# An attention and MLP-mixer kernel: the second batch's loads issued ahead of Pool's casts, its copy of v on VectorE, and the first lists rearranged

## The chip, the cores and the metric

The kernel runs on one core of a Trainium2 chip. The metric is the device time of one execution in microseconds (us). The kernel before took 351.95 us, the median of three runs (349.81 to 352.16). Engines are named as in the profile: PE is TensorE (PEld its weight loads), DVE is VectorE, ACT is ScalarE, POOL is GpSimd, SP is the engine that in this kernel only issues DMAs. In the traces of this case each engine works through its own list of instructions in order, and an instruction that waits holds up all that stand behind it in that list: below, a copy on Pool whose input was ready at 21.9 us starts at 52.65 us, behind the list ahead of it, and holds PE's list for 21.4 us.

## The reference, cut to what matters

```python
def _attn_ref(q, k, v, global_idx):            # q, k, v: (8, 8, 576, 64) float32
    scores = scale * np.matmul(q, k.transpose(0, 1, 3, 2))
    mask = np.abs(pos[:, None] - pos[None, :]) <= 32
    mask = mask | is_global[:, None] | is_global[None, :]      # 8 global tokens
    scores = np.where(mask, scores, -1000000000.0)
    ...                                         # softmax over the row
    return np.matmul(attn, v)

def _moe_ref(x, w_tok1, w_tok2, w_ch1, w_ch2):  # x: (8, 576, 512)
    h = np.maximum(xt @ w_tok1, 0.0) @ w_tok2   # token mixer, xt = x transposed
    u = x + h.transpose(0, 2, 1)
    h2 = np.maximum(u @ w_ch1, 0.0) @ w_ch2     # channel MLP, 512 -> 1536 -> 512
    return u + h2
```

There are eight batches. Each goes through attention, the token mixer and the channel MLP.

## The kernel before

The kernel is a hand-made schedule. The order of the calls in the text is the order of each engine's list. Batch 0 runs alone at first (the start-up). From then on the channel MLP of batch b, which is dense work for PE, is mixed with the attention and token mixer of batch b+1 and the first steps of batch b+2. The first such stretch is "period 0": the channel MLP of batch 0, the attention of batch 1, the transposes of batch 2.

v is kept twice, as `vsh` and, shifted by 64 rows, as `vod` (the "odd copy"), because every second tile of 64 rows needs the shifted one. The helpers:

```python
    def load_v16(b):
        for c in range(NT):
            r0, r1, j0 = vrows(c)
            nc.gpsimd.dma_start(
                out=vsh[b % 2][r0:r1, c, :, 0:D],
                in_=v[b, :, j0 : j0 + (r1 - r0), :].rearrange("h p d -> p h d"),
            )

    def v_odd(b, hs=slice(0, H), eng=nc.gpsimd):
        i = b % 2
        eng.tensor_copy(out=vod[i][HQ:P, :, hs], in_=vsh[i][HQ:P, 0 : NT - 1, hs])
        eng.tensor_copy(out=vod[i][0:HQ, :, hs], in_=vsh[i][0:HQ, 1:NT, hs])

    def castv(p):
        hs = slice(2 * p, 2 * p + 2)
        nc.gpsimd.tensor_copy(out=vsh[0][:, :, hs, 0:D], in_=lv[:, :, hs])

    def cast_qk(b, ti, p, eng):

        if p is None:
            eng(out=(qr, kr)[ti][b % 2], in_=(lqr, lkr)[ti])
        else:
            hs = slice(2 * p, 2 * p + 2)
            eng(out=(qn, kn)[ti][b % 2][:, :, hs].rearrange("p i h d -> p h i d"), in_=(lq, lk)[ti][:, hs])
```

For batch 0 the work goes by pairs of heads. `PV0(p)` multiplies the weights of pair p with v, and needs `castv(p)` and the odd copy of that pair:

```python
    def PV0(p):
        s = st[0]
        ps = (pss if p % 2 else psv)([P, 2, 512], name=f"pv0_{p}")
        st[0]["pv", p] = ps
        spots = [(t, 64 * (t % 2)) for t in range(2 * NT - 1)] + [(2 * NT - 2, 64)]
        for t, r0 in spots:
            tau = t // 2
            lo = QS * tau + (NG + HQ if t % 2 else NG)
            for par in range(2):
                nc.tensor.matmul(
                    ps[r0 : r0 + 64, par, VW * tau : VW * tau + VW], lhsT=e_all[:, 2 * p + par, lo : lo + HQ],
                    rhs=(vod if t % 2 else vsh)[0][:, tau, 2 * p + par, :], start=t < 2, stop=False,
                )
        # ... the global part, out of lf and rf
```

The end of the batch-0 lists as the kernel before has them, with the block of Pool work for batch 1 in the middle. The odd copy of pair 3 (heads 6 and 7) stands behind that block in the text, but it is on VectorE, whose list has nothing of the block:

```python
    castv(2)
    load_wc1(0)
    v_odd(0, slice(2, 4), nc.vector)
    OG0(0)
    SX(0, 3, 1)
    OG0(1)
    RF0(0)
    v_odd(0, slice(4, 6), nc.gpsimd)
    LM(0)
    SX(0, 3, 0)
    OG0(2)
    RF0(2)
    PV0(0)
    RF0(1)
    castv(3)
    nc.gpsimd.memset(w2[:, :, S:], 0.0)
    load_wc1(4)
    load_wc1(8)
    load_qk1()
    load_wc2(0)
    qk_pads(1)
    v_ones(1)
    v_rows(1)
    x_pads(1)
    for p in (None, 0, 1, 2, 3):
        cast_qk(1, 0, p, G)
        cast_qk(1, 1, p, G)
    load_wc2(4)
    load_wc2(8)
    load_v16(1)
    v_odd(1)
    gather(1)
    PV0(1)
    NO0(0)
    OG0(3)
    v_odd(0, slice(6, 8), nc.vector)
    PV0(2)
    RF0(3)
    NO0(1)
    PV0(3)
    M1_0(0)
    NO0(3)
    M1_0(1)
    RU0(0)
    NO0(2)
    M2_0(0)
    RU0(1)
    # ... the rest of batch 0's token mixer, UT0(3), UT0(2), M2(0, 2), masks_a()
```

In period 0, `D` stands for the next unit of batch 0's channel MLP (`M4` is four b1p matmuls, `M5` six op matmuls), n is batch 1, m is batch 2:

```python
    def period_0():
        n, m = 1, 2
        D = None
        c2 = casts(m)
        u = [D, D, D, D, D, lambda: TR(n), D, lambda: globals_(n), lambda: t(n, 0), D]
        u += [lambda: t(n, 1), D, s2(n, 0), D, lambda: t(n, 2), lambda: SM(n, 0), D, s2(n, 1), D, lambda: t(n, 3)]
        u += [lambda: SM(n, 1), s2(n, 2), D]
        u += [D, lambda: SM(n, 2), lambda: GK(n), s2(n, 3), D, lambda: (load_rest(m), load_qk(m, slice(0, H)))]
        u += [lambda: SM(n, 3), D, lambda: OG(n), D, lambda: PV(n, 0), D, lambda: PV(n, 1), D]
        u += [lambda: PV(n, 2), lambda: [M1(n, ch) for ch in range(2)], lambda: PV(n, 3), D]
        u += [lambda: PV(n, 4), lambda: M1(n, 2), D, lambda: [M1(n, ch) for ch in range(3, NT)], *c2]
        u += [lambda: (M2(n, 0), M3(n, 0)), lambda: (M2(n, 1), M3(n, 1)), lambda: (M2(n, 2), M3(n, 2))]
        u += [lambda: (load_v16(m), v_odd(m)), lambda: globals_(m), lambda: TR(m)]
        u += [lambda p=p: t(m, p) for p in range(NP)]
        return u
```

The softmax here doesn't subtract the row's maximum and nothing guards it: scores larger than these inputs give would overflow.

## Time and profile before

| what | us | view |
|---|---|---|
| span of the profiled run | 351.7 | page |
| PE busy | 314.0 (89%) | busy time of each engine |
| first b1p matmul: batch 0's channel MLP starts, period 0 begins | 34.6 | timeline, PE |
| first b1p matmul of batch 1: period 0 ends | 89.2 | timeline, PE |

PE bounds the kernel: it is busy for 89% of the span and makes up 73% of the chain that ended last (page). Most of what can be saved lies in the first 90 us: in the table by stages PE is idle for about 24 us there, of 38 us in the whole span. These are lines of the page: busy share of 40 slices of 8.8 us in tenths, and under PEclk the clock granted to PE, in tenths of full speed.

```profile
PE 314.0 (89%) x3431; PEld 168.2 (48%) x3431; DVE 182.6 (52%) x380; ACT 154.4 (44%) x276; POOL 95.7 (27%) x125
...
PE   4799986773899999799998999899989999999993
...
POOL 8995564855204400530035000430000000000000
PEclk9589999997699999989999999999999999999999
```

PE's digits fall to 6, 7, 7 and 3 in the seventh to tenth slice (53 to 88 us), and the clock falls to 0.7 and 0.6 in the tenth and eleventh. The view of waits says for what. Its columns are: who waited, for whom, us in total, times, longest.

```profile
PE pT L398 <- DVE kT L436: 7.0, 5, 1.7
PE b1p L738 <- DMA uT<-u: 4.7, 1, 4.7
PE s L456 <- ACT kT L410: 2.6, 1, 2.6
PE warm L205 <- POOL ident masks.py:199: 2.0, 1, 2.0
PE pv L663 <- POOL vod L372: 1.9, 1, 1.9
```

Pool's timeline shows where batch 1 comes from. Columns: start, length, engine, line, instruction, and in brackets the idle time before it and what ended it.

```profile
26.39 0.94 POOL L367 DMA_DIRECT2D lk<-in_k_dram  x1
...
34.32 0.40 POOL L381 CAST qr<-lqr 128x256 f16<-128x256 f32 x1 [3.63 <-DMA lqr<-in_q_dram]
37.83 0.40 POOL L381 CAST kr<-lkr 128x256 f16<-128x256 f32 x1 [3.11 <-DMA lkr<-in_k_dram]
...
40.43 0.61 POOL L384 CAST kn<-lk 128x512 f16<-128x512 f32 x1 [1.64 <-DMA lk<-in_k_dram]
...
45.80 4.22 POOL L359 DMA_DIRECT2D vsh<-in_v_dram  x5
57.02 2.24 POOL L371 COPY vod<-vsh 64x2112 f16<-64x2112 f16 x1 [7.00 <-DMA vsh<-in_v_dram]
59.32 1.94 POOL L372 COPY vod<-vsh 64x2112 f16<-64x2112 f16 x1
```

Each cast runs as soon as its load has landed, from 34 us on. v of batch 1 is issued last and landed at 57 us, and Pool then copies it for 4 us while PE waits 1.9. At the end of period 0, PE waits 4.7 us for the DMA transposes of u. And the odd copy of batch 0's pair 3 is on VectorE, early:

```profile
26.36 0.48 DVE L371 COPY vod<-vsh 64x528 f16<-64x528 f16 x1
26.88 0.55 DVE L372 COPY vod<-vsh 64x528 f16<-64x528 f16 x1
```

### The profile page before, as it was taken

How to read it: one execution, taken by the hardware profiler on the slowest of the kernel's cores; microseconds unless marked ns; L12 is line 12 of the kernel's file. 1: busy time of each engine (PE TensorE's matmuls, PEld its weight loads, DVE VectorE, ACT ScalarE, POOL GpSimd, SP SyncE). 2: the span in 40 equal slices, each digit the busy share in tenths (PEclk: the TensorE clock that was granted, in tenths of full speed). 3: DMA queues.
4: the chain of work that ended last, by engine and by line, in shares of the span. 5: the costliest groups of instructions: out<-in, count | busy, mean ns of one | idle time of the engine just before them, and what ended most of it. 6: DMA issues, size and time to landing. Idle time of an engine off the chain costs nothing.

```text
span 351.7 us, 8081 instructions
## 1 busy us (share of the span) xinstructions
PE 314.0 (89%) x3431; PEld 168.2 (48%) x3431; DVE 182.6 (52%) x380; ACT 154.4 (44%) x276; POOL 95.7 (27%) x125
## 2 busy tenths in 40 slices
PE   4799986773899999799998999899989999999993
PEld 4468443432346554445454644444445645444641
DVE  5578464456244676556647474576656464241021
ACT  3654572051466335543365442563466433413600
POOL 8995564855204400530035000430000000000000
PEclk9589999997699999989999999999999999999999
DMA  7899699999909782929293922949100312042012
GB/s 212 190 178 264 162 130 158 289 91 137 260 10 89 199 203 63 88 43 302 77 108 38 278 91 63 99 147 227 62 2 15 76 63 61 0 104 91 0 67 85
DMA packets 82022, 42.37 MB, mean 120 GB/s; under 512 B 56578, under 2 KB 76674, under 8 KB 81986
## 3 DMA queue, kind: packets, MB, share of 16 engines
q1 hardware_dynamic: 43944, 31.20, 32.9%
q0 software_dynamic: 37904, 10.52, 28.2%
q8 instruction: 27, 0.44, 0.6%
q10 hardware_dynamic: 138, 0.13, 0.1%
q14 instruction: 9, 0.07, 0.1%
HBM read 36.11 MB, written 9.44 MB: 130 GB/s over the span
## 4 chain that ended last, share of the span: by engine, by line
PE 73%; DMA 9%; DVE 7%; POOL 7%; issue 2%; ACT 1%; SPq 0%; another core or an unknown queue 0%; POOLq 0%; ACTq 0%
PE op L764 25%; PE b1p L738 22%; PE a1p L690 4%; PE hp L710 4%; DMA lk<-in_k_dram 4%; PE s L456 4%; PE pv L654 3%; PE b1lp L751 3%; PE pT L398 3%; PE pv L663 2%; DMA vsh<-in_v_dram 2%; DMA uT<-u 2%; DVE x L677 2%; POOL kn L384 1%; PE og L537 1%
## 5 line engine op out<-in xcount | busy, mean ns | idle before, releaser
L738 PE MATMUL b1p<-uT,wc 128*128 128x512 f16 x384 | 97.6, 388 | 4.7 <-DMA uT<-u 4.7
L741 ACT ACTIVATE b<-b1p 128x512 f16<-128x512 f32 x96 | 56.9, 598 | 93.8 <-PE b1p L738 93.5
L764 PE MATMUL op<-wc,b 128*128 128x512 f16 x384 | 89.8, 380 | 0.0
L468 ACT ACTIVATE e_all<-s 128x544 f16<-128x544 f32 (+1 forms) x64 | 41.1, 685 | 40.7 <-issue 32.2
L359 POOL DMA_DIRECT2D vsh<-in_v_dram x35 | 29.5, 863 | 105.2 <-PE pv L663 98.2
L738 PEld LDWEIGHTS <-wc 128*128 128x128 f16 x384 | 34.8, 99 | 42.6 <-issue 8.3
L764 PEld LDWEIGHTS <-b 128*128 128x128 f16 x384 | 35.2, 98 | 38.9
L768 DVE TENSOR_TENSOR osb<-u,op 128x512 f32<-128x512 f16 x32 | 22.0, 687 | 55.1 <-PE op L764 52.5
L404 DVE COPY qT<-pT 128x512 f16<-128x512 f16 x31 | 21.3, 687 | 13.6 <-PE pT L398 12.7
L676 DVE RECIPROCAL rr<-pv 128x8 f32<-128x8 f32 (+1 forms) x35 | 7.3, 207 | 39.3 <-PE pv L663 36.6
L715 DVE TENSOR_TENSOR u<-x,hp 128x1024 f16<-128x1024 f16 x14 | 17.0, 1220 | 18.6 <-PE hp L710 18.6
L456 PE MATMUL s<-qT,kT 64*64 64x136 f16 (+2 forms) x704 | 19.0, 226 | 7.2 <-ACT kT L410 2.6
L479 DVE TENSOR_TENSOR e_all<-e_all,bandm 128x616 f16<-128x616 f16 x56 | 24.3, 476 | 1.0
L677 DVE TENSOR_TENSOR x<-pv,rr 128x512 f16<-128x512 f32 (+1 forms) x35 | 24.2, 691 | 1.2
L456 PEld LDWEIGHTS <-kT 64*64 64x64 f16 x704 | 12.2, 111 | 22.0 <-issue 16.1
L654 PE MATMUL pv<-rf,lf 128*64 128x264 f16 x126 | 19.1, 288 | 2.6 <-DVE x L677 1.8
L398 PE MATMUL pT<-ident,qn 128*128 128x128 f16 x128 | 13.3, 231 | 8.6 <-DVE kT L436 7.0
L710 PE MATMUL hp<-a,w 128*128 128x512 f16 x72 | 18.8, 379 | 1.6 <-ACT a L694 1.2
L663 PEld LDWEIGHTS <-e_all 128*64 128x64 f16 x504 | 18.5, 111 | 2.2 <-issue 2.1
L371 POOL COPY vod<-vsh 64x2112 f16<-64x2112 f16 (+1 forms) x8 | 14.5, 1816 | 17.6 <-DMA vsh<-in_v_dram 17.4
L410 DVE COPY kT<-pT 128x512 f16<-128x512 f16 x28 | 19.1, 681 | 0.0
L663 PE MATMUL pv<-vsh,e_all 128*64 128x66 f16 x280 | 18.8, 194 | 0.0
(170 smaller groups left out, 374.1 us busy)
## 6 DMA issues: line engine op xcount, KB each, us to landing
out_dram<-osb SPq DMA_DIRECT2D x32, 256.0 KB
lq<-in_q_dram SPq DMA_DIRECT2D x6, 1024.0 KB
lk<-in_k_dram SPq DMA_DIRECT2D x6, 1024.0 KB
wc<-in_moe_w_ch_dram POOLq DMA_DIRECT2D x6, 512.0 KB, 9.8
vsh<-in_v_dram POOLq DMA_DIRECT2D x21, 128.0 KB, 5.1
vsh<-in_v_dram POOLq DMA_DIRECT2D x14, 96.0 KB, 3.1
lq<-in_q_dram SPq DMA_DIRECT2D x4, 256.0 KB
lk<-in_k_dram SPq DMA_DIRECT2D x4, 256.0 KB
```

What stands on the lines that cost most here:

```text
L359: nc.gpsimd.dma_start(out=vsh[b % 2][r0:r1, c, :, 0:D], in_=v[b, :, j0 : j0 + (r1 - r0), :].rearrange("h p d -> p h d"),)
L398: nc.tensor.transpose(out=pT[:, ti, P * i : P * i + P], in_=n[b % 2][:, i, 2 * p : 2 * p + 2, :], identity=ident)
L456: nc.tensor.matmul(ps[o, par, i0 - a : i1 - a], lhsT=kT[r, HQ * j : HQ * j + HQ], rhs=qf[r, i0:i1], start=b > 0, stop=b > 0 or j in js[-2:],)
L468: nc.scalar.activation(out=e2[:, :, a:z], in_=ps[:, :, 0 : z - a], func=AF.Exp, scale=scale)
L479: nc.vector.tensor_mul(out=e2[:, par], in0=e2[:, par], in1=bm)
L654: nc.tensor.matmul(ps[r0 : r0 + 64, hf, 0 : NP * VW], lhsT=s["lf"][:, HQ * t : HQ * t + HQ], rhs=s["rf"][:, 2 * hf : 2 * hf + 2], start=Tr ...
L663: nc.tensor.matmul(ps[r0 : r0 + 64, hf, VW * hh : VW * hh + VW], lhsT=e_all[:, h, lo : lo + HQ], rhs=(vod if t % 2 else vsh)[b % 2][:, tau ...
L677: nc.vector.tensor_tensor(out=x16s[b % 2][r, tau, :].rearrange("p (f h x) -> p f h x", f=2, h=NP), in0=pq[r, :, :, 0:D], in1=rr[r].unsquee ...
L710: nc.tensor.matmul(ps[:, i, :], lhsT=w2[:, ch, P * tau - sh : P * tau - sh + P], rhs=s["a1"][:, ch, :], start=(ch == 0), stop=(ch == 1),)
L738: nc.tensor.matmul(ps, lhsT=wc1[:, cc, P * j : P * j + P], rhs=s["uT"][:, cc, :], start=(cc == 0), stop=(cc == 3))
L741: nc.scalar.activation(out=s["b1"][:, j, :], in_=ps, func=AF.Relu)
L764: nc.tensor.matmul(ps, lhsT=w, rhs=wc2[:, j, :], start=(j == 0), stop=(j == NJ - 1))
```

## The change

Its intent, as it was described: issue the second batch's loads early from Pool, ahead of its casts; do that batch's copy of v on VectorE; rearrange the first lists around data that arrives late. The core of the diff (cut; the start-up lists were reordered throughout, several memsets went from Pool to VectorE, some PSUM pools were swapped, and the odd copy of pair 2 went from Pool to VectorE, while that of pair 3 went the other way):

```diff
     load_qk1()
     load_wc2(0)
-    qk_pads(1)
+    load_wc2(4)
+    load_wc2(8)
     v_ones(1)
     v_rows(1)
+    load_v16(1)
     x_pads(1)
+    qk_pads(1)
     for p in (None, 0, 1, 2, 3):
         cast_qk(1, 0, p, G)
         cast_qk(1, 1, p, G)
-    load_wc2(4)
-    load_wc2(8)
-    load_v16(1)
-    v_odd(1)
     gather(1)
-    PV0(1)
-    NO0(0)
-    OG0(3)
-    v_odd(0, slice(6, 8), nc.vector)
-    PV0(2)
+    PV0(0)
+    NO0(1)
+    v_odd(0, slice(6, 8), nc.gpsimd)
+    OG0(3)
     # ... cut; PE: PV0(1), PV0(0), OG0(3), M1_0(1), PV0(3), M1_0(0), PV0(2), ...
```

And in period 0:

```diff
-        u += [D, lambda: SM(n, 2), lambda: GK(n), s2(n, 3), D, lambda: (load_rest(m), load_qk(m, slice(0, H)))]
-        u += [lambda: SM(n, 3), D, lambda: OG(n), D, lambda: PV(n, 0), D, lambda: PV(n, 1), D]
+        u += [D, lambda: SM(n, 2), lambda: GK(n), s2(n, 3), D, lambda: SM(n, 3), D, D, D]
+        u += [lambda: v_odd(n, eng=nc.vector), lambda: OG(n), D, lambda: (load_rest(m), load_qk(m, slice(0, H)))]
+        u += [lambda: PV(n, 0), lambda: PV(n, 1), D, lambda: PV(n, 2), lambda: PV(n, 3), D]
         # ... cut
+        u += [lambda: (M2(n, 0), M3(n, 0)), lambda: (M2(n, 1), M3(n, 1)), lambda: globals_(m), lambda: TR(m), lambda: t(m, 0)]
+        u += [lambda: (M2(n, 2), M3(n, 2)), lambda: (load_v16(m), v_odd(m)), lambda: t(m, 1), s2(m, 0), lambda: t(m, 2)]
+        u += [lambda: SM(m, 0), lambda: t(m, 3), s2(m, 1), lambda: SM(m, 1)]
```

More of the change, by code (lines that the diff above doesn't have):

```diff
@@ L119, in load_rest @@
         for ten, dst in ((q, lqr), (k, lkr)):
-            (nc.scalar if b == 0 and ten is q else nc.sync).dma_start(out=dst.rearrange("p i d -> p (i d)"), in_=rest_src(ten, b))
+            nc.sync.dma_start(out=dst.rearrange("p i d -> p (i d)"), in_=rest_src(ten, b))
     def load_v0(p):
@@ L134 @@
         load_qk(0, slice(2 * p, 2 * p + 2))
-        if p == 0:
+        if p == 1:
             load_rest(0)
@@ L158, in qk_pads @@
     def qk_pads(i):
-        nc.gpsimd.memset(kTs[i][:, :, 0:WIN], 0.0)
-        nc.gpsimd.memset(kTs[i][:, :, WIN + S :], 0.0)
+        nc.vector.memset(kTs[i][:, :, 0:WIN], 0.0)
+        nc.vector.memset(kTs[i][:, :, WIN + S :], 0.0)
     qk_pads(0)
-    nc.gpsimd.memset(qTs[0][:, :, :, 0:NG], 0.0)
+    nc.vector.memset(qTs[0][:, :, :, 0:NG], 0.0)
+    nc.vector.memset(lv[0:WIN, 0], 0.0)
+    nc.vector.memset(lv[P - WIN : P, NT - 1], 0.0)
     def int_op(name, s, op, s2=None, op2=ALU.bypass):
@@ L276 @@
     nc.gpsimd.iota(it_i, pattern=[[1, S]], base=0, channel_multiplier=0)
-    nc.gpsimd.memset(lv[0:WIN, 0], 0.0)
-    nc.gpsimd.memset(lv[P - WIN : P, NT - 1], 0.0)
     e_all = const.tile([P, H, ES], F16)
@@ L287, in v_ones, with v_rows @@
         nc.gpsimd.memset(vsh[i][:, :, :, D : D + 1], 1.0)
-    def v_rows(i):
-        nc.gpsimd.memset(vsh[i][0:WIN, 0], 0.0)
-        nc.gpsimd.memset(vsh[i][P - WIN : P, NT - 1], 0.0)
+    def v_rows(i, eng=nc.gpsimd):
+        xs = slice(D, D + 1) if i == 0 else slice(0, VW)
+        eng.memset(vsh[i][0:WIN, 0, :, xs], 0.0)
+        eng.memset(vsh[i][P - WIN : P, NT - 1, :, xs], 0.0)
     def x_pads(i):
@@ L394, in T @@
     def T(b, p):
-        pT = (psm if b == 0 else pss)([P, 2, 512], F16, name=f"pT_{b}_{p}")
+        pT = (psm if b in (0, 2) else pss)([P, 2, 512], F16, name=f"pT_{b}_{p}")
         for ti, n in enumerate((qn, kn)):
@@ L419, in TR @@
     def TR(b):
-        pr = (psm if b == 0 else pss)([P, 2, 4, NP * 16], name=f"pr_{b}")
+        pr = (psm if b in (0, 2) else pss)([P, 2, 4, NP * 16], name=f"pr_{b}")
         sel = ident.rearrange("p (n r x) -> p r n x", n=NP, r=2)
@@ L507, in GK @@
         s = st[b]
-        ps = (psv if b == 0 or b > 2 else pss)([P, 2, 512], name=f"gk_{b}")
+        ps = (psv if b != 2 else pss)([P, 2, 512], name=f"gk_{b}")
         for p in range(NP):
@@ L533, in OG @@
         s = st[b]
-        ps = (psv if b > 2 else pss)([P, 2, VW], name=f"og_{b}")
+        ps = (psv if b != 2 else pss)([P, 2, VW], name=f"og_{b}")
         for c in range(NT):
@@ L549, in OG0 @@
         s = st[0]
-        if p == 0:
+        if "rf" not in s:
             s["rf"] = mb.tile([P, NP, 2, VW], F16, tag="rf", name="rf_0")
@@ L600, in M1_0 @@
         s = st[0]
-        if p == 0:
+        if "a1" not in s:
             s["a1"] = mb.tile([P, 2, DM], F16, tag="a1", bufs=1, name="a1_0")
@@ L649, in PV @@
         tiles = ((2 * tau, 0), (2 * tau + 1, 64)) if tau < NT - 1 else ((2 * tau, sh),)
-        ps = (pss if b > 2 and tau % 2 else psv)([P, 2, 512], name=f"pv_{b}_{tau}")
+        ps = (pss if b != 2 and tau % 2 else psv)([P, 2, 512], name=f"pv_{b}_{tau}")
         def glob(hf):
@@ L786, in sparse2 @@
         u = [(0.0, lambda: (load_rest(n), load_qk(n, slice(0, H))))]
-        for p in range(NP):
+        for p in (2, 3):
             u += [(0.3, lambda p=p: S_(b, p, 0)), (1.8, lambda p=p: S_(b, p, 1)), (0.0, lambda p=p: SM(b, p))]
@@ L827, in period_0 @@
         u += [lambda: SM(n, 1), s2(n, 2), D]
-        u += [D, lambda: SM(n, 2), lambda: GK(n), s2(n, 3), D, lambda: (load_rest(m), load_qk(m, slice(0, H)))]
-        u += [lambda: SM(n, 3), D, lambda: OG(n), D, lambda: PV(n, 0), D, lambda: PV(n, 1), D]
-        u += [lambda: PV(n, 2), lambda: [M1(n, ch) for ch in range(2)], lambda: PV(n, 3), D]
-        u += [lambda: PV(n, 4), lambda: M1(n, 2), D, lambda: [M1(n, ch) for ch in range(3, NT)], *c2]
-        u += [lambda: (M2(n, 0), M3(n, 0)), lambda: (M2(n, 1), M3(n, 1)), lambda: (M2(n, 2), M3(n, 2))]
-        u += [lambda: (load_v16(m), v_odd(m)), lambda: globals_(m), lambda: TR(m)]
-        u += [lambda p=p: t(m, p) for p in range(NP)]
+        u += [D, lambda: SM(n, 2), lambda: GK(n), s2(n, 3), D, lambda: SM(n, 3), D, D, D]
+        u += [lambda: v_odd(n, eng=nc.vector), lambda: OG(n), D, lambda: (load_rest(m), load_qk(m, slice(0, H)))]
+        u += [lambda: PV(n, 0), lambda: PV(n, 1), D, lambda: PV(n, 2), lambda: PV(n, 3), D]
+        u += [lambda: PV(n, 4), lambda: [M1(n, ch) for ch in range(NT)], *c2]
+        u += [lambda: (M2(n, 0), M3(n, 0)), lambda: (M2(n, 1), M3(n, 1)), lambda: globals_(m), lambda: TR(m), lambda: t(m, 0)]
+        u += [lambda: (M2(n, 2), M3(n, 2)), lambda: (load_v16(m), v_odd(m)), lambda: t(m, 1), s2(m, 0), lambda: t(m, 2)]
+        u += [lambda: SM(m, 0), lambda: t(m, 3), s2(m, 1), lambda: SM(m, 1)]
         return u
@@ L880 @@
     A, V, G = nc.scalar.copy, nc.vector.tensor_copy, nc.gpsimd.tensor_copy
+    consts()
     W(10)
@@ L884 @@
     W(20)
-    consts()
-    cast_qk(0, 0, 0, A)
-    cast_qk(0, 1, 0, A)
-    cast_qk(0, 0, None, V)
+    cast_qk(0, 0, 0, V)
+    cast_qk(0, 0, 1, A)
+    cast_qk(0, 1, 0, V)
+    gather(0, (0,))
+    masks_b()
+    masks_c()
     T(0, 0)
+    TEq(0, 0, A)
+    cast_qk(0, 1, None, A)
+    TEk(0, 0, A)
+    cast_qk(0, 1, 1, V)
     gather(0, (1,))
-    masks_c()
-    TEq(0, 0, V)
-    TEk(0, 0, A)
-    cast_qk(0, 0, 1, A)
-    cast_qk(0, 1, 1, V)
+    v_ones(0)
+    nc.gpsimd.memset(w1l, 0.0)
+    v_rows(0, nc.vector)
+    cast_qk(0, 0, 2, V)
+    cast_qk(0, 0, None, A)
+    T(0, 1)
+    masks_d()
+    cast_qk(0, 1, 2, A)
+    TR(0)
+    TEq(0, 1, V)
+    TEk(0, 1, A)
     S_(0, 0, 0)
+    TRE(0, (0,), A)
+    TRE(0, (1,), V)
+    S_(0, 1, 0)
     SX(0, 0, 0)
-    gather(0, (0,))
-    v_ones(0)
-    v_rows(0)
-    nc.gpsimd.memset(w1l, 0.0)
-    T(0, 1)
-    cast_qk(0, 0, 2, V)
-    masks_b()
-    TEk(0, 1, A)
-    TEq(0, 1, A)
-    cast_qk(0, 1, None, A)
-    S_(0, 1, 0)
-    cast_qk(0, 1, 2, G)
-    TR(0)
-    masks_d()
-    SX(0, 1, 0)
-    G(out=g16[1][0], in_=g32[1][0])
-    T(0, 2)
-    TRE(0, (1,), V)
-    TRE(0, (0,), A)
-    castv(0)
+    G(out=g16[0][0], in_=g32[0][0])
+    T(0, 2)
+    load_w1()
+    load_w1l()
+    load_w2()
+    SX(0, 1, 0)
     S_(0, 1, 1)
-    TEq(0, 2, V)
-    TEk(0, 2, A)
+    TEk(0, 2, V)
     S_(0, 0, 1)
@@ L923 @@
     cast_qk(0, 0, 3, V)
-    G(out=g16[0][0], in_=g32[0][0])
-    load_w1()
-    load_w1l()
-    load_w2()
     cast_qk(0, 1, 3, V)
+    SX(0, 0, 1)
+    TEq(0, 2, V)
+    T(0, 3)
+    G(out=g16[1][0], in_=g32[1][0])
+    TEq(0, 3, A)
+    TEk(0, 3, V)
+    S_(0, 2, 0)
+    castv(0)
     gather_t(0)
-    SX(0, 0, 1)
-    S_(0, 2, 0)
+    S_(0, 2, 1)
+    SX(0, 2, 0)
     GTE(0)
+    castv(1)
     GKE(0)
-    T(0, 3)
-    SX(0, 2, 0)
-    v_odd(0, slice(0, 2), nc.vector)
-    S_(0, 2, 1)
-    TEk(0, 3, A)
-    TEq(0, 3, V)
     SX(0, 2, 1)
     GQ0()
-    castv(1)
+    v_odd(0, slice(0, 2), nc.vector)
+    v_odd(0, slice(2, 4), nc.vector)
     GK(0)
@@ L950 @@
     load_wc1(0)
-    v_odd(0, slice(2, 4), nc.vector)
-    OG0(0)
     SX(0, 3, 1)
     OG0(1)
-    RF0(0)
-    v_odd(0, slice(4, 6), nc.gpsimd)
-    LM(0)
-    SX(0, 3, 0)
-    OG0(2)
-    RF0(2)
-    PV0(0)
-    RF0(1)
+    LM(0)
+    OG0(0)
+    RF0(1)
+    SX(0, 3, 0)
+    v_odd(0, slice(4, 6), nc.vector)
+    OG0(2)
+    PV0(1)
+    RF0(2)
+    RF0(0)
     castv(3)
@@ L975 @@
         cast_qk(1, 1, p, G)
-    load_wc2(4)
-    load_wc2(8)
-    load_v16(1)
-    v_odd(1)
     gather(1)
-    PV0(1)
-    NO0(0)
-    OG0(3)
-    v_odd(0, slice(6, 8), nc.vector)
-    PV0(2)
-    RF0(3)
-    NO0(1)
+    PV0(0)
+    NO0(1)
+    v_odd(0, slice(6, 8), nc.gpsimd)
+    OG0(3)
+    RF0(3)
+    M1_0(1)
+    NO0(0)
     PV0(3)
+    RU0(1)
     M1_0(0)
     NO0(3)
-    M1_0(1)
+    PV0(2)
     RU0(0)
+    M2_0(0)
     NO0(2)
-    M2_0(0)
-    RU0(1)
     M1_0(3)
     M2_0(1)
+    RU0(3)
     AD0(0)
-    RU0(3)
     M1_0(2)
@@ L1005 @@
     AD0(3)
+    M2_0(2)
+    UT0(0)
     M3_0(1)
-    UT0(0)
-    M2_0(2)
+    AD0(2)
     UT0(1)
-    AD0(2)
     M3_0(3)
```

## The prediction

> **What bounds it now.** TensorE: busy 314.0 of 351.7 us (engine table); the chain of waits is 73% PE. From about 100 us on there is little idle. The slack lies in the start-up (batch 0 alone, up to the first channel-MLP matmul at 34.6 us in the timeline) and in period 0 (34.6 to 89.2 us, where the second batch's channel MLP starts). In period 0 the timeline shows 1.9 us waiting for Pool's copies of v (57.0 to 61.3 us, two of about 1.94 us), batch 2's transposes at VectorE's pace (78.7 to 84.5 us), 4.7 us waiting for the DMA transposes of u, then some 5 us at a granted clock of 0.72 to 0.77 (stage table).
>
> **What the change intends.** v of batch 1 (landed only at 57 us) is issued before Pool's casts; its odd copy goes to VectorE; batch 2's transposes and first scores fill the wait for the u transposes. This should recover roughly 2 us (Pool copy) plus 5 to 8 us (u wait, clock dip, transposes).
>
> **What I think it breaks.** The last odd copy of batch 0's v (pair 3) was on VectorE, at 26.4 us. Now it is on Pool, behind everything for batch 1: the wc2 and v loads, ten casts, four gathers. Pool runs in order, and PE's in-order list needs this copy for PV0(3), before the rest of batch 0's mixer. Waits ahead of it in Pool's list: [...] the copy for the gathers to land.
>
> Costs from the trace: k of batch 1 is issued at 26.4 us and lands at 40.4; Pool skips about 5 us of small work but VectorE's memsets delay the gather index, so perhaps 39 us now. Casts: 5.3 us, to about 45. Bytes: the wc2 loads and v (4.3 MB read) follow k; two wc2 loads plus v took 44.3 to 57 us, about 255 GB/s, so wc2 lands near 50 and v near 55. Gathers took about 4.5 us to land: 55 to 57. Copy 1.3 us: PV0(3) can finish near 57.5 us instead of 28.
>
> PE is then idle from roughly 26 to 57 us. In before, PV0(3) to first channel-MLP matmul took 7.1 us; I allow 8[...]. [...] So that matmul moves from 34.6 to about 65.5 us. Period 0 then finds its data: I estimate 45 to 47 us instead of 54.6, including 1.5 us of batch 2's scores moved in. The second batch's channel MLP starts near 111 instead of 89.2; minus the moved work and the vanished clock dip, net about +18 us. All after is PE-bound and unchanged, so this is nearly all critical.
>
> **Prediction:** 370 us, 8 in 10 between 359.5 and 381. Faster by over 2%: 0.04; within 2%: 0.07; slower by over 2%: 0.89.
>
> **What would show it.** Right: PE idle 20 to 30 us, released by Pool's 64x528 vod copy; that copy after the casts and gathers, at 50 us or later; first b1p matmul after 57 us; period 0 under 50 us; no 4.7 us wait for uT. Wrong: the vod copy or the first b1p matmul before 45 us.
>
> **What would make it wrong.** [...] period 0 compressing more once its data is there; or a longer stall, if gathers are served slowly after all v packets.

The copy's end near 57.5 us (gathers landed at 55 to 57, plus 1.3; that the gathers come only after the landings of wc2 and the first of v is the author's estimate, with its reason cut) plus 8 is 65.5 us for the first b1p. With 45 to 47 us of period 0 that gives about 111 instead of 89.2, or +22; less the moved work (1.5) and the clock dip (it has no figure of its own; about 2 is what is left for it), +18; and 352 + 18 is 370 us.

## The result, and the profile after

The changed kernel took 374.99 us (median of 4 runs, 372.39 to 376.37) against 350.88 us for the kernel before in the same rounds (349.57 to 352.16). The ratio is 1.068, with a 95% interval of 1.060 to 1.076. Ratios here are the mean time of one kernel's fast runs over the mean of the other's fast runs in the same rounds, so not quite the ratio of the quoted medians. The output is correct.

The same lines of the page, now for slices of 9.3 us:

```profile
PE 318.1 (86%) x3431; PEld 173.5 (47%) x3431; DVE 186.0 (50%) x393; ACT 153.4 (41%) x275; POOL 87.7 (24%) x113
...
PE   5695019989858998997999899989998999999994
...
POOL 6885755301240350035003500250000000000000
PEclk9999999999989999999999999999999999999999
```

PE has a hole (0 and 1) in the fifth and sixth slice that was not there before. The waits of PE name it:

```profile
PE pv L578 <- POOL vod L373: 21.4, 1, 21.4
PE pT L399 <- DVE kT L437: 6.3, 4, 1.7
PE pT L399 <- ACT kn L385: 3.9, 1, 3.9
```

The 4.7 us wait for uT and the 1.9 us wait for the full odd copy are gone, as intended. One wait of 21.4 us has come. Pool's timeline shows how it arises:

```profile
25.75 0.92 POOL L368 DMA_DIRECT2D lk<-in_k_dram  x1
...
35.88 1.77 POOL L360 DMA_DIRECT2D vsh<-in_v_dram  x2 [1.70 <-DMA lq<-in_q_dram]
39.48 0.78 POOL L360 DMA_DIRECT2D vsh<-in_v_dram  x1 [1.83 <-DMA lk<-in_k_dram]
...
40.77 0.40 POOL L382 CAST qr<-lqr 128x256 f16<-128x256 f32 x1
...
50.04 0.94 POOL L236 DMA_INDIRECT g_k<-in_k_dram,idx_i  x1 [0.30 <-issue]
52.65 0.62 POOL L372 COPY vod<-vsh 64x528 f16<-64x528 f16 x1 [1.66 <-DMA g_k<-in_k_dram,idx_i]
53.33 0.62 POOL L373 COPY vod<-vsh 64x528 f16<-64x528 f16 x1
```

The copy of pair 3, 1.3 us of work whose input was cast by 21.9 us, starts at 52.65 us. Everything for batch 1 stands ahead of it. Two things in that list are worth a look. Pool stood idle for 1.83 us before the last issue of v, and the trace puts that down to the landing of k, which this issue does not read; the 1.70 us before the two issues ahead of it are put down to q in the same way. Why an issue of v waits for them is in no trace. The casts behind these issues, whose first input had landed at 34 us in the kernel before, therefore start only at 40.8 us. And the trace puts the last 1.66 us of idle time before the copy down to the gathers' data, although the copy reads none of it.

PE's timeline on both sides of the hole:

```profile
32.31 0.32 PE L578 MATMUL pv<-vsh,e_all 128*64 128x66 f16 x2
54.00 0.21 PE L578 MATMUL pv<-vod,e_all 128*64 128x66 f16 x1 [21.37 <-POOL vod L373]
```

and the two b1p matmuls that mark the ends of period 0, with the wait before the second:

```profile
64.80 4.52 PE L739 MATMUL b1p<-uT,wc 128*128 128x512 f16 x20
...
106.21 0.50 PE L399 MATMUL pT<-ident,kn 128*128 128x128 f16 x4 [3.92 <-ACT kn L385]
112.10 1.04 PE L739 MATMUL b1p<-uT,wc 128*128 128x512 f16 x4
```

| stretch | before | after | difference |
|---|---|---|---|
| start to first b1p | 34.6 | 64.8 | +30.2 |
| period 0 | 89.2 - 34.6 = 54.6 | 112.1 - 64.8 = 47.3 | -7.3 |
| the rest of the span | 351.7 - 89.2 = 262.5 | 370.6 - 112.1 = 258.5 | -4.0 |
| span of the profiled run | 351.7 | 370.6 | +18.9 |

So the new period 0 does gain: 7.3 us in itself, and 4.0 us in the rest. (The rest probably gains because some of batch 2's scores are already done, and because no slow clock follows: the record of the kernel before is 0.77 between 90 and 100 us, right after its period 0, that of the changed kernel 1.00 between 110 and 140 us. Neither share was measured.) The start-up loses 30.2 us, of which the hole is 21.4. The other 8.8 us do not come from the hole: e1 below has no hole, and its first b1p still comes 9.0 us later than in the kernel before. The profiled run, at 372.39 us, was also the fastest of the four. By the medians the loss is 24.1 us; what the slower runs lose beyond the table's 18.9 us is in no trace.

### The profile page after: what moved, and what is told of

It reads as the page before. It is cut to its first block, busy times and chain, and to the rows that moved or that the text cites. A ratio compares the mean times of both kernels' runs of the same rounds, so it can differ in the third digit from the quotient of the medians.

```text
span 370.6 us, 8086 instructions
## 1 busy us (share of the span) xinstructions
PE 318.1 (86%) x3431; PEld 173.5 (47%) x3431; DVE 186.0 (50%) x393; ACT 153.4 (41%) x275; POOL 87.7 (24%) x113
## 4 chain that ended last, share of the span: by engine, by line
PE 71%; DVE 4%; issue 4%; DMA 3%; ACT 2%; SPq 1%; ACTq 0%
PE op L765 23%; PE b1p L739 22%; PE hp L711 4%; PE a1p L691 4%; DMA lk<-in_k_dram 3%; PE s L457 3%; PE pT L399 3%; PE b1lp L752 3%; PE pv L655 3%; PE pv L664 2%; DVE x L678 1%; PE a1p L612 1%; ACT e_all L469 1%; PE og L538 1%; PE hp L625 1%
## 5 line engine op out<-in xcount | busy, mean ns | idle before, releaser
L739 PE MATMUL b1p<-uT,wc 128*128 128x512 f16 x384 | 94.7, 380 | 0.5 <-ACT b L742 0.5
L411 DVE COPY kT<-pT 128x512 f16<-128x512 f16 x30 | 20.4, 680 | 1.5 <-PE pT L399 0.8
L578 PE MATMUL pv<-vod,e_all 128*64 128x66 f16 x32 | 2.6, 245 | 21.4 <-POOL vod L373 21.4
L655 PE MATMUL pv<-rf,lf 128*64 128x264 f16 x126 | 18.9, 287 | 0.9 <-DVE kgz L354 0.7
```

The costliest lines, as they stand in the source:

```text
L655: nc.tensor.matmul(ps[r0 : r0 + 64, hf, 0 : NP * VW], lhsT=s["lf"][:, HQ * t : HQ * t + HQ], rhs=s["rf"][:, 2 * hf : 2 * hf + 2], start=Tr ...
L739: nc.tensor.matmul(ps, lhsT=wc1[:, cc, P * j : P * j + P], rhs=s["uT"][:, cc, :], start=(cc == 0), stop=(cc == 3))
```

## The experiments

The theory: the time is lost because the odd copy of pair 3 stands on Pool behind the work for batch 1. The rivals: the early loads disturb the loads that matter; the new start-up lists or VectorE's memsets are slow in themselves; Pool is simply too slow an engine for the copy. All twelve kernels gave the right output. The kernel before was run beside each. "Median" is over all runs of the kernel; the ratio uses fast runs alone. One run of the kernel before, in the rounds of e5 to e8, took 1687.22 us; it counts as slow and is in no ratio. The profiled runs of e2, e8, e11 and e12 are slow.

| run | what it is | median us (before, same rounds) | ratio, 95% interval |
|---|---|---|---|
| e1 | changed kernel, pair-3 copy back on VectorE | 353.59 (352.33) | 0.996, 0.984 to 1.008 |
| e2 | changed kernel, copy on Pool but early in its list | 353.62 (352.33) | 1.003, 0.994 to 1.011 |
| e3 | changed kernel, copy just ahead of the gathers | 370.15 (352.33) | 1.048, 1.036 to 1.060 |
| e4 | kernel before, only the copy moved to Pool | 384.73 (352.33) | 1.088, 1.078 to 1.098 |
| e5 | e1, batch 2's load at its old place | 349.96 (351.08) | 0.998, 0.993 to 1.002 |
| e6 | e1, more warm-up matmuls | 351.81 (351.08) | 1.003, 1.000 to 1.007 |
| e7 | old start-up, early loads, new period 0, batch 2's load at its old place | 348.92 (351.08) | 0.997, 0.992 to 1.001 |
| e8 | kernel before, early loads and VectorE copy only | 350.80 (351.08) | 1.001, 0.996 to 1.006 |
| e9 | e7, v issued after the casts | 342.63 (352.05) | 0.973, 0.967 to 0.980 |
| e10 | e8, v issued after the casts | 345.08 (352.05) | 0.983, 0.977 to 0.989 |
| e11 | changed kernel, PE kept busy in the hole | 374.05 (352.05) | 1.061, 1.051 to 1.070 |
| e12 | e5, v issued after the casts | 347.69 (351.38) | 0.976, 0.969 to 0.984 |

### e1 to e4: is it the place of one copy?

e1, one word:

```diff
-    v_odd(0, slice(6, 8), nc.gpsimd)
+    v_odd(0, slice(6, 8), nc.vector)
```

> The changed kernel with one word undone: the odd copy of batch 0's v for heads 6 and 7 goes back to VectorE. Theory (the copy's place in Pool's queue is the cause): the 21.4 us wait of PE for Pool's vod copy vanishes, the first b1p matmul moves from 64.8 us to 40 to 44 us, and the time falls to about 350 us (345 to 355), level with the kernel before, because the rest of the change still loses a little in the start-up and in the 3.9 us wait for batch 2's k. Rival (the early loads of wc2 and v, or the memsets put on VectorE, slow the first 60 us by contention): the time stays above 360 us.

e2, the same copy on Pool, moved up:

```diff
     castv(3)
+    v_odd(0, slice(6, 8), nc.gpsimd)
     nc.gpsimd.memset(w2[:, :, S:], 0.0)
     # ...
     NO0(1)
-    v_odd(0, slice(6, 8), nc.gpsimd)
```

> The changed kernel; the copy for heads 6 and 7 stays on Pool but stands right behind the cast of its own v, ahead of the loads for batch 1. Theory (place in the queue, not the engine): same time as the run with the copy on VectorE, within 3 us, since it costs Pool only 1.3 us. Rival (Pool is the wrong engine for this copy): the time stays within 5 us of the changed kernel, 370 us or more.

e3, moved up past the gathers only:

```diff
         cast_qk(1, 1, p, G)
+    v_odd(0, slice(6, 8), nc.gpsimd)
     gather(1)
     PV0(0)
     NO0(1)
-    v_odd(0, slice(6, 8), nc.gpsimd)
```

> The changed kernel; the copy for heads 6 and 7 moves up past the four gathers only, still behind the loads and casts of batch 1. Theory: the copy starts when the casts end, near 46 us instead of 52.65, so the time falls by about 6.5 us, to 368 us; every microsecond of the copy is a microsecond of the kernel. Rival (the copy is held by the v loads and not by its place): no change, 374 us.

e4, the kernel before with the opposite one-word edit (`nc.vector` to `nc.gpsimd` in the same call):

> The kernel before with one word changed: the copy for heads 6 and 7 goes to Pool at the place where the text has it, behind the casts, the loads, the full odd copy of batch 1 and the gathers. Theory: PE waits for it until about 71 us instead of 28; period 0 then finds its data and shrinks from 54.6 to about 45 us; the time rises by 30 to 38 us, to about 385 us. Rival (the word is harmless and the new order of lists or the early loads did the damage): less than 358 us.

Measured: e1 and e2 are both level with the kernel before. Moving this one copy undoes the whole net loss of 6.8%, and the engine is not the reason: on Pool, early in the list, it costs the kernel no more than on VectorE (1.003 against 0.996, with intervals that overlap). In e1 the 21.4 us wait is gone and the first b1p matmul stands at 43.6 us. In e3 the copy starts at 45.30 us, 7.35 us earlier than in the changed kernel, and PE's wait is 7.4 us shorter:

```profile
45.30 0.62 POOL L372 COPY vod<-vsh 64x528 f16<-64x528 f16 x1
45.99 0.62 POOL L373 COPY vod<-vsh 64x528 f16<-64x528 f16 x1
```

```profile
PE pv L578 <- POOL vod L373: 14.0, 1, 14.0
```

How far the time fell is not sharp, because the two kernels ran in different rounds: the medians fell by 4.8 us (374.99 to 370.15), the ratios by 2.0 points (1.068 to 1.048), which is about 7 us. A fall of 6.5 was expected, and both agree with it within the intervals. In the profiled run the first b1p came only 5.1 us earlier (59.67 against 64.80), since PE then took 13.0 us instead of 10.8 from its restart to that matmul. So "every microsecond of the copy is a microsecond of the kernel" is not shown. e4 rose by 32.4 us (384.73 - 352.33), inside the 30 to 38 that were expected, with this wait of PE:

```profile
PE pv L577 <- POOL vod L372: 41.4, 1, 41.4
```

As causes of the net loss the rivals fall. The early loads, memsets and lists of e1 are those of the changed kernel, and it does not lose. That its start-up costs nothing is not shown: it ends 9.0 us later than in the kernel before, and the rest of the kernel makes up for that.

### e5 and e6: what still eats the gain once the copy is mended?

e1 has the shorter period 0 and is still only level. Two suspects stood in its profile: PE waits 4.2 us for ACT's cast of batch 2's k, and the start-up ends at 43.6 instead of 34.6 us.

e5, on top of e1:

```diff
-        u += [D, lambda: SM(n, 2), lambda: GK(n), s2(n, 3), D, lambda: SM(n, 3), D, D, D]
-        u += [lambda: v_odd(n, eng=nc.vector), lambda: OG(n), D, lambda: (load_rest(m), load_qk(m, slice(0, H)))]
+        u += [D, lambda: SM(n, 2), lambda: GK(n), s2(n, 3), D, lambda: (load_rest(m), load_qk(m, slice(0, H))), lambda: SM(n, 3), D, D, D]
+        u += [lambda: v_odd(n, eng=nc.vector), lambda: OG(n), D]
```

> The changed kernel with the pair-3 copy on VectorE, and with the load of batch 2's q and k put back to the place where the kernel before has it (ahead of the last mask of period 0, not behind the copy and the global output). Theory: the 4.2 us wait of PE for ACT's cast of batch 2's k is the load being issued late (k issued about 12 us before it lands); it vanishes and the time falls by 3 to 5 us against the run with the copy on VectorE, to about 349.5 us. Rival (that wait only hides another, VectorE's or the DMA transposes): less than 1.5 us gained.

e6, on top of e1:

```diff
-    W(10)
+    W(32)
     indices()
     # ...
     S_(0, 0, 0)
+    W(22)
     TRE(0, (0,), A)
```

> The changed kernel with the pair-3 copy on VectorE, and with 44 more warm-up matmuls in two waits of the start-up (22 before the index matmul, 22 while PE waits for the second k transpose). Theory [...]: the batch-0 matmuls take about 0.20 instead of 0.25 us from 15 us on, the first b1p matmul moves from 43.6 us to 37 to 39 us, the time falls by 4 to 6 us, to about 348.5 us. Rival (the slow clock costs nothing because VectorE and ACT set the pace there): b1p moves by less than 1.5 us.

Measured for e5: the wait is gone from the profile, and batch 1's channel MLP starts at 88.7 instead of 94.2 us. The time, 349.96 us, is what was expected, but the ratio of 0.998 overlaps that of e1, so a gain over e1 is not shown by the timed runs. In the changed kernel the load stands behind two more writes of the output in SP's list, and k is issued 12 us before the cast of it starts; in the kernel before, 17 us (58.99 to 76.18).

Measured for e6 (`W(n)` issues n matmuls whose result nobody reads): the matmuls were faster. These lines are the last `pv<-rf` group of batch 0 and the first b1p matmuls, from e1 and from e6:

```profile
35.59 0.87 PE L586 MATMUL pv<-rf,lf 32*128 32x66 f16 x12
43.57 2.80 PE L739 MATMUL b1p<-uT,wc 128*128 128x512 f16 x12
```

```profile
30.92 0.60 PE L586 MATMUL pv<-rf,lf 32*128 32x66 f16 x12
36.30 4.52 PE L739 MATMUL b1p<-uT,wc 128*128 128x512 f16 x20
```

The same twelve matmuls take 0.87 us in e1 and 0.60 in e6, and the first b1p comes 7.3 us earlier (36.3 against 43.6). So batch 0 had run at a slow clock in e1: in e3 such groups of 0.87 us stand beside a clock record of 0.50 (20 to 30 us), in the kernel before those of 0.60 us beside one of 1.00 (20 to 30 us). What made it slow is not shown; the expectation's statement on batch 0's clock and its cause is cut. That the added matmuls made the others faster is not shown either. e11 below has the changed kernel's PE list, without them, up to its filler. Its trace and the changed kernel's agree within 0.03 us for each matmul up to 18 us; then, by the length of its groups, one runs at the full clock and the other does not. These are the first such groups of the changed kernel and of e11:

```profile
28.18 0.87 PE L586 MATMUL pv<-rf,lf 32*128 32x66 f16 x12
```

```profile
25.31 0.60 PE L586 MATMUL pv<-rf,lf 32*128 32x66 f16 x12
```

So the same list can run at either clock, and e1 and e6 have one trace each. The time did not follow in e6: 351.81 us, ratio 1.003. PE now reached batch 1's data before Pool had cast it, and waited 1.5 us for the cast of q's rest and still 3.9 for batch 2's k; batch 1's channel MLP started 5.1 us earlier in the profiled run (89.1), and that run was the fastest of the six. Why the timed runs do not show those 5 us is open; that some of e1's other runs had the full clock too would explain it, but none of them has a trace.

### e7 to e10: the parts of the change on the old start-up

e7 keeps the start-up of the kernel before and takes the rest of the change, with the load of batch 2 where it was:

```diff
-    qk_pads(1)
+    load_wc2(4)
+    load_wc2(8)
     v_ones(1)
     v_rows(1)
+    load_v16(1)
+    qk_pads(1)
     x_pads(1)
     # ... the ten casts
-    load_wc2(4)
-    load_wc2(8)
-    load_v16(1)
-    v_odd(1)
     gather(1)
     # and period_0() as in e5, with the PSUM pools that it needs
```

> The kernel before, its start-up lists kept; only the early loads on Pool, the copy of batch 1's v on VectorE and the new period 0 are taken from the change, with the load of batch 2 at its old place. Theory (the new start-up order is what eats the gain of the new period): first b1p at 34.6 us as before, batch 1's channel MLP starts at 80 to 83 us instead of 89.2, and the time is 343 to 347 us, better than both kernels. Rival (the early loads or the new period 0 lose as much as they gain): 350 us or more.

e8 makes the same edit to Pool's list and puts `v_odd(n, eng=nc.vector)` ahead of `OG(n)`, with the lists of period 0 as they were:

> The kernel before with only the early loads of wc2 and v on Pool and the copy of batch 1's v on VectorE; both lists as before. Theory: PE's 1.9 us wait for Pool's copy of v vanishes, the 4.7 us wait for the DMA transposes of u stays; 349 to 351 us, 1 to 3 us below the kernel before. Rival (v issued before the casts delays the casts of batch 1, and period 0 with them): same or slower than before.

e7 missed its expectation (0.997). e8's 350.80 us lies in the expected 349 to 351, but the expected gain over the kernel before is absent (1.001), which is what its rival said. The profile of e7 says why. PE has a new wait of 4.0 us for Pool's cast of the rest of q, and Pool's timeline shows what holds that cast:

```profile
36.66 1.75 POOL L359 DMA_DIRECT2D vsh<-in_v_dram  x2 [2.39 <-DMA lq<-in_q_dram]
40.59 0.78 POOL L359 DMA_DIRECT2D vsh<-in_v_dram  x1 [2.18 <-DMA lk<-in_k_dram]
...
42.28 0.40 POOL L381 CAST qr<-lqr 128x256 f16<-128x256 f32 x1
```

The last issue of v came only when k had landed, after 2.18 us of idle time, and the casts stand behind it. v itself is issued earlier (at 32 to 41 instead of 46 to 50 us), but the casts come 8 us later (34.32 to 42.28). Hence e9, which is e7 with this:

```diff
     v_ones(1)
     v_rows(1)
-    load_v16(1)
     # ...
         cast_qk(1, 1, p, G)
+    load_v16(1)
     gather(1)
```

> As the run with the old start-up and the new period 0, but on Pool batch 1's v is issued after the ten casts (the wc2 loads still before them). Theory (the v issues block Pool until k has landed, one after the other, and so hold the casts of q that could have run earlier): PE's 4.0 us wait for Pool's cast of the rest of q falls below 1 us; v still lands before the copy on VectorE needs it; batch 1's channel MLP starts at 82 to 84 us instead of 86.6; 344 to 347 us, and clear of the kernel before by over 1%. Rival (the wait is for the landing of q itself, or v now lands too late): no gain over the run with v before the casts (0.997 of before).

and e10, which is e8 with the same edit:

> As the last, with the lists of period 0 left as the kernel before has them: only the two wc2 loads move ahead of the casts, v follows the casts directly, and the copy of batch 1's v is on VectorE. Theory: the 5.9 us wait for the cast of the rest of q falls below 1 us; the 1.9 us wait for Pool's copy is gone; the 4.7 us wait for the transposes of u stays; 348 to 350 us. If it equals the run with the new period, the new lists of period 0 are worth nothing.

e9 took 342.63 us against 352.05, a ratio of 0.973: the best version found, better than both kernels, though its interval reaches just over 0.980. Pool's timeline in e9 has the first cast back at its load's landing and v issued right behind the casts:

```profile
33.82 0.40 POOL L381 CAST qr<-lqr 128x256 f16<-128x256 f32 x1 [0.53 <-DMA lqr<-in_q_dram]
...
43.87 4.20 POOL L359 DMA_DIRECT2D vsh<-in_v_dram  x5
```

The copy of v on VectorE then takes 1.4 us, where Pool took 4, and PE no longer waits for it:

```profile
59.03 0.71 DVE L371 COPY vod<-vsh 64x2112 f16<-64x2112 f16 x1
59.77 0.70 DVE L372 COPY vod<-vsh 64x2112 f16<-64x2112 f16 x1
```

Batch 1's channel MLP starts at 79.83 us, 9.4 earlier than in the kernel before, and the time is 9.4 us lower (352.05 - 342.63). e10, at 0.983, did better than expected (345.08 instead of 348 to 350 us). So moving the two wc2 loads ahead of the casts, v right behind them and the copy to VectorE is worth 1.7%; the new lists of period 0 add about 1 point on top, a difference that the two intervals just leave open.

### e11: does the slow clock after the hole cost anything?

```diff
     NO0(0)
+    fill = psm([P, P], name="fill")
+    for _ in range(320):
+        nc.tensor.matmul(fill, lhsT=ident, rhs=ident, start=True, stop=True)
     PV0(3)
```

> The changed kernel as it is, with 320 warm-up matmuls put into PE's list right where it waits 21.4 us for the copy. Theory (part of the loss is that batch 0's rest runs at half clock after the idle time): the stretch from the copy to the first b1p matmul, 10.8 us, falls to 7 to 8 us, and the time to about 371.5 us. Rival (the rest of batch 0 is paced by VectorE and ACT): under 1 us gained.

Inconclusive for the time. The filler was over at 45.8 us in the profiled run, PE then idled 8.3 us, and the matmuls behind the hole were as slow as before, with a clock record of 0.50 between 50 and 60 us:

```profile
54.92 0.87 PE L586 MATMUL pv<-rf,lf 32*128 32x66 f16 x12
```

The same groups had taken 0.60 us ahead of the filler in this run, so here idle time of PE was followed by a slow clock. In the changed kernel it need not have been the hole: there the groups take 0.87 us at 28.18 us already, before it. The time, ratio 1.061 against 1.068, is not apart from the changed kernel's. What the slow clock costs there can be read from e1 and e6, which have the same PE list in this stretch: from the last `pv<-rf` group to the first b1p matmul, 43.57 - 35.59 = 8.0 us in e1 and 36.30 - 30.92 = 5.4 us in e6.

### e12: is the new start-up to blame?

e12 is e5 with the edit of e9, so that it differs from e9 in the start-up alone.

> The changed kernel with all three defects mended: the pair-3 copy on VectorE, the load of batch 2 at its old place, v of batch 1 after the ten casts on Pool. It differs from the best version so far (2.7% below the kernel before) in the start-up lists, memsets and first loads alone. Theory (the new start-up lists are the part of the change that loses once the copy is mended, because the first b1p matmul comes at 43 to 44 us instead of 35): no better than the run with two defects mended, 349 to 351 us, a ratio to before of 0.99 to 1.00; casts-first gains nothing here, since batch 1's transposes are not asked for before 48 us. Rival (the start-up lists cost little and v's place did it all): 344 us or less.

The expectation was missed. The ratio of the fast runs is 0.976, and that is not apart from e9. The seven runs fall into two groups: three at 341.57 to 342.25 us, and four at 347.69 to 349.84, which count as slow. In these three fast runs the new start-up is as good as the old one, so the theory that it must eat the gain fell. But a run is called slow here because it is over 1.5% above the fastest of its kernel; over all seven runs the mean is 345.8 us, against 350.8 for the kernel before. The profiled run was a slow one (first b1p at 42.8 us, matmuls of 0.87 us as in e1). That the fast runs are those in which PE gets its full clock early is a guess, since none of them has a trace. It fits that e11's trace shows the changed kernel's start-up list at the full clock, and that the means of the two groups lie 6.8 us apart, near the 7.3 us by which the first b1p of e6 precedes that of e1. The clocks do not settle it: 0.988 to 0.993 in the fast runs; 0.950, 0.951, 0.969 and 0.994 in the slow ones. If the guess holds, leaving the slow runs out flatters the new start-up. What stays open is also how much of e5's 350 us, in runs that are all called fast by their own kernel's best, was this same slow start.

## Why the prediction was right

- **The step that carried it held.** The prediction said that the copy of pair 3 on Pool stands "behind everything for batch 1" and that PE waits for it "20 to 30 us". PE waited 21.4 us; with the copy back (e1, e2), the loss was gone. Alone in the kernel before (e4), the same word cost 32.4 us.
- **The queue was longer in the sum than in fact.** Predicted: gathers landing at 55 to 57 us and PV0(3) able to finish near 57.5. Measured: the copy began at 52.65 and PE went on at 54.0. The landing of wc2 was put too late: "near 50". Its three loads took 14.9 to 16.8 us from issue, the last of them from 29.87 us, so all had landed by about 47. The gathers, which the prediction put after it, were issued from 46.1 us on, and of the 0.16 to 0.31 us of idle time before each of them the trace puts none down to a load.
- **The rest of batch 0 was underrated.** "I allow 8": from PE's restart to the first b1p it took 64.8 - 54.0 = 10.8 us. Part is the slow clock (8.0 against 5.4 us for a piece of it in e1 and e6). Another part may be the new order, in which PE waits before PV0(3) with the mixer steps of pairs 0 and 2 and PV0(2) still to do; this was not measured apart. The two errors nearly cancel, which is luck: 64.8 us against the predicted 65.5.
- **Period 0** was 47.3 us against "45 to 47". It held a 3.9 us wait for batch 2's k, which the prediction did not see: the load had moved behind two more output writes in SP's list. With the load moved back (e5) the wait is gone, and period 0 took 88.7 - 43.9 = 44.8 us.
- **The gain that the change meant to have** ("roughly 2 us plus 5 to 8 us") is real: e9 has 9.4 us of it. But the change as written did not have it even with the copy mended (e1). e7 (0.997) and e8 (1.001) show that v ahead of the casts costs what it brings. The prediction counted waits ahead of the issues of v to time the copy; it did not count what later casts cost batch 1.
- **The clock.** The prediction allowed 8 us because it took PE to be slow after idle time. e11 shows one such case: its groups took 0.60 us before 8.3 us of idle time and 0.87 us after it, with the record at 1.00 from 20 to 40 us and at 0.50 from 50 to 60. But the slow clock was not the hole's doing in the changed kernel, whose groups took 0.87 us before the hole already. Its clock record does not show this; see the last section.
- **Total.** 370 was predicted, 374.99 measured, inside the range. As a difference, +18 us was predicted: the profiled runs differ by 18.9, the medians by 24.1. The close match with the profile owes something to luck, for that run was the fastest of four.

## What to carry to other kernels

Before moving an operation to another engine, read that engine's whole list up to the place where it lands: a copy of 1.3 us held PE for 21.4 us because it stood behind work that waited for loads of another batch. In these traces a DMA issue that waited delayed all that stood behind it: in e7 the last issue of v came after 2.18 us of waiting for the load of k, and the casts behind it began at 42.28 us, where the same cast of q began at 34.32 in the kernel before, as soon as its data was there. Putting v after the casts, with nothing else changed, turned a change worth nothing (e7) into 2.7% (e9). When a large rearrangement loses, undo its smallest suspicious part first: one word separated 1.068 from 0.996.

## What the clock records, the DMA issues and the copies of this case show

- In e3 (a fast run) PE was busy for 9.71 of 10 us between 20 and 30 us, in mostly small matmuls, and the granted clock stayed at 0.50; the groups of twelve took 0.87 us there, so the record can be believed. What sets the clock is in no trace, so this shows only that the profile's busy share does not foretell the clock. The line is from the table by stages (us, then PE, PEld, DVE, ACT, POOL busy, then PEclk, DMA share and GB/s):

```profile
20.00:30.00 10.00, 9.71 (x183) 6.14 (x182) 6.41 (x21) 4.36 (x8) 7.92 (x14) 0.50 1.17 196
```

- Clock records can be wrong: the changed kernel's record says 1.00 from 0 to 100 us, with matmul groups of 0.87 us that take 0.60 at full clock, and e1's says 1.00 up to 50 us in the same way. The length of a repeated group of matmuls told the clock where the record did not.
- Issues of v on Pool waited for older loads that they do not read: 1.7 and 1.8 us in the changed kernel, and in e7 the casts behind them came about 8 us later (42.28 against 34.32 us). Why they wait is in no trace.
- VectorE made the copies of 2112 f16 elements in e9 in 0.71 and 0.70 us. Pool took 2.24 and 1.94 us for the same copies in the kernel before.
